# First two gate blocks on unscaled x, and a new order of events for chunks 0 and 1, in a linear attention, SwiGLU and rational kernel

## The chip, the cores and the metric

The kernel runs on one core of a Trainium2 chip. The metric is the device time of one execution in microseconds (us). Engines: PE is TensorE (matrix products), DVE is VectorE, ACT is ScalarE, POOL is GpSimd, SP is the queue of SyncE, which issues all transfers here.

## The reference

Three stages in a row, all in float32 (some inputs arrive as float64). First a linear attention over 4 batches, 8 heads, 576 positions, head size 64; then a SwiGLU block on 2304 tokens of 512 channels; then a block with a rational function.

```python
q_s = softmax(q, axis=-1); k_s = softmax(k, axis=2)
kv  = einsum('bhsd,bhse->bhde', k_s, v)
x   = einsum('bhsd,bhde->bhse', q_s, kv)      # -> [2304, 512]
rms = sqrt(mean(x * x, axis=-1) + 1e-06)
xn  = x / rms * rms_g
g   = xn @ w_gate;  val = xn @ w_val          # 512 -> 1536
y   = (g * sigmoid(g) * val) @ w_out          # 1536 -> 512
h   = y @ w_in                                # 512 -> 2048
g2  = (a0 + a1 h + a2 h^2 + a3 h^3) / (1 + |b0||h| + |b1|h^2 + 1e-06)
out = g2 @ w_out2                             # 2048 -> 512
```

## The kernel before, in words

The 2304 tokens are worked in six chunks of 384 (T). For every chunk the attention gives x, transposed, as four blocks of 128 channels; then 12 blocks f of 128 hidden channels follow, each with a gate product (g), a value product (v), Silu, the multiplication (p), and an output product (y) that adds to four PSUM banks. The results y of all chunks are parked in HBM, and after the last chunk the rational stage runs over all of them. PE does nothing but products.

Weights arrive as float64 bytes. Each weight block i (36 of them: gate, value and output of 12 blocks f) is loaded (event `l`, line 144), turned into float32 by two ACT passes (`ce`, line 181, `cl`, line 189) and a DVE join (`cj`, line 196), then split for the three-pass products into a high half (`ch`: line 219 on ACT, or line 217 on DVE for the blocks listed in HI_DVE) and a low half (`co`, line 226, on DVE, or on POOL for the blocks in LO_POOL). A product from split halves is three matmuls per 128 channels (`proj`, lines 725 to 727). In chunk 0 the gate and value products of the first NF = 4 blocks and the output products of the first NY = 8 use the joined float32 weight whole (`proj_whole`, line 738, and `y_whole`, line 754), so that they can start before the halves are made.

The events of chunks 0 and 1 stand in ORDER, a list written out by hand at the top of the file. Every name is a small function (`put`, `bank`, `reader`, from line 944 on), and each engine works its own events in the order of the list. Events of chunk 0 begin with `a`: `alk`, `alq`, `alv` load k, q, v; `akm`, `akt`, `akx`, `aks`, `akd`, `ake` are the maximum of k over the positions, its transposes and its subtraction, and the exponential; `akv` is the product of k and v (72 small matmuls) and `akn` its division; `aqm`, `aqd`, `aqe`, `aqs`, `aqn` do the softmax of q, the subtraction and the division in two halves; `axq`, `axc`, `axx` turn q and multiply it with kv for channel block p; `axo` copies x to SBUF, `axs` squares it, `arp` sums the squares over channels on PE, `arn` computes 1/rms for every token in 14 DVE instructions (`rms`, lines 574 to 593), `arb` spreads it over the partitions with a product into a PSUM bank (line 623), and `axm` (line 634) multiplies x by g and by that bank. Only then can `g0_0` begin. Events `b` and `d` are the same for the chunks 1 and 2. Events `w8`, `w9`, `w4` are groups of 8, 9 and 4 matmuls on the identity (line 936) whose result is not used.

OTHER lists events that run on the engine other than the usual one (DVE instead of POOL or ACT, or the reverse). The function `rms` and the helper lines carry the same line numbers for all chunks. PSUM has four banks (`pw`) that all `bank` events share, and four (`pa`) for y. The gate tiles `u` have two buffers, as have `uh`, `ul` and `tmp`. SP issues transfers strictly in order, so a load whose buffer is still read holds back all loads behind it: `blk1` waits for the last reader of the turned q of chunk 0, `blq` for the last `arp`, and the loads of blocks 28 to 35 for the whole weights whose buffers they take.

Of the kernel before, what the change touches and what calls it, by code (L numbers as in the profile page):

```python
# [27 lines left out]
ORDER = """
alk0 akz1 bkz1 akz0 bkz0 alq akm0 alk1 w8 akt0 alv0 akx0 aqm aks0 akd0 aqd0 alv1 ake0 aqd1 akm1 aqe w9 akv0 lg aqs l0
akt1 l1 akx1 akn0 aqn0 w4 aks1 l3 ce0 akd1 aqn1 axq1 axq0 l11 ake1 cl0 axq2 axc2 akv1 l2 cj0 axc0 axc1 ce3 ce1 l16 cl1  # L30
axx0 akn1 axx1 axs0 l4 axq3 axs1 arp0 axo0 axo1 l7 axc3 axx2 cj1 axx3 ce2 axs2 l10 arp1 axs3 ce4 arp2 axo3 blk1 axo2
arp3 cl2 arn cl4 blq ce7 ce10 ce11 ce16 cj2 w8 arb l8 cl3 axm0 axm1 axh0 l25 axm2 axh1 axm3 w4 g0_0 axh2 l19 axl1 axh3
axl0 ce8 axl2 l5 cl10 axl3 v0_0 s0_0 l9 cl7 g0_1 l15 cl16 p0_0 cj10 ce5 cj16 cl5 l21 cj4 s0_1 cj7 y0_0 ce9 l6 ce15
cl15 l13 cj3 cl9 cj5 cl11 v0_1 l12 cl8 ce6 cj11 blv0 cl6 cj15 g0_2 p0_1 ch15 ce13 co15 ce12 cj8 y0_1 s0_2 blk0 cl12
ch11 l18 cl13 cj6 ch0 co11 v0_2 ce19 l14 ch1 co0 ce21 cj9 pk0 g0_3 ch2 p0_2 ce18 cl18 lc ce14 cj12 y0_2 l20 s0_3 cj13
cl14 ch12 l17 ch13 v0_3 const co1 ch5 l23 cj14 ce20 co12 ch14 g0_4 co5 pk1 cl19 p0_3 bkm0 ce17 co14 cl17 l35 y0_3 s0_4
ce23 cj19 l24 ch10 cl21 cj18 bkt0 l26 v0_4 co13 ch18 cj17 ch4 l27 co18 ch3 g0_5 p0_4 ch17 bkm1 cl20 co4 l22 v0_5 s0_5
co10 l33 ce26 bqm ce27 co3 y0_4 l30 ce22 p0_5 cl26 co17 cl22 pk3 ce25 y0_5 ch8 bkx0 ce30 cj22 ce24 co2 bks0 ch22 bkt1
cj20 pk2 ch16 g0_6 bkx1 ch20 bqd0 bkd0 ch7 l34 bks1 s0_6 co20 v0_6 bke0 cl23 co7 g0_7 p0_6 ce34 bkd1 bqd1 ch6 y0_6
s0_7 bke1 cj23 bkv0 cj21 ch9 co6 ch23 co9 blv1 ch21 bkn0 co22 bqe co21 cl24 bqs co23 v0_7 cl27 l32 ce33 co8 cl30 g0_8  # L40
p0_7 ch19 bqn0 l31 cl25 cl33 co19 bxq0 s0_8 bkv1 cj25 bxc0 ce31 bxx0 cj27 ce32 bxq1 cj24 bxs0 y0_7 bkn1 bqn1 bxc1 ch24
bxo0 co24 ch27 v0_8 cl31 co27 ch25 cl32 bxx1 co16 ce35 p0_8 bxq2 ph0_8 bxc2 pl0_8 l29 bxs1 bxx2 cj26 bxo1 bxq3 bxa1
ch26 cj30 bxc3 co26 bxs2 bxx3 ch30 bxa2 g0_9 ce29 co25 cl29 co30 l28 s0_9 cj29 bxs3 bxo2 bxo3 v0_9 bxa3 ch29 cj32 ce28
co29 cl28 brp p0_9 g0_10 ph0_9 ch32 pl0_9 cj28 v0_10 s0_10 brn co32 ch28 co28 g0_11 p0_10 y0_8 s0_11 cj31 brb cj33
ph0_10 ch31 pl0_10 ch33 bxm0 co31 bxm1 bxh0 bxh1 bxl0 y0_9 bxm2 co33 bxm3 bxh2 bxl1 bxh3 v0_11 bxl2 bxl3 g1_0 p0_11
dlq cl34 ph0_11 pl0_11 v1_0 s1_0 cl35 cj34 g1_1 p1_0 ch34 dqm co34 v1_1 s1_1 cj35 y0_10 dqd0 ch35 p1_1 dqd1 g1_2 ph1_0
co35 dqe pl1_0 y0_11 s1_2 dqs v1_2 ph1_1 ye0_2 g1_3 ye0_1 p1_2 ye0_0 pl1_1 ye0_3 ly0 v1_3 s1_3 y1_0 p1_3 y1_1 ph1_2
dqn0 pl1_2 dxq0 ph1_3 y1_2 dxc0 pl1_3 dqn1 dxx0 dxq1 dxs0 y1_3 dxc1 dxo0 dxx1 dxq2 dxs1 g1_4 dxc2 dxa1 dxo1 dxx2 s1_4
dxq3 dxs2 v1_4 dxc3 dxa2 dxo2 g1_5 p1_4 ph1_4 pl1_4 dxx3 s1_5 y1_4 dxs3 dxo3 dxa3 drp v1_5 drn g1_6 p1_5 ph1_5 drb
s1_6 v1_6 pl1_5 dxm0 dxm1 dxh0 y1_5 dxh1 p1_6 dxl0 ph1_6 pl1_6 g1_7 dxm2 dxm3 dxh2 dxl1 dxh3 y1_6 s1_7 dxl3 dxl2 v1_7  # L50
g1_8 p1_7 ph1_7 pl1_7 v1_8 s1_8 y1_7 p1_8 ph1_8 pl1_8 g1_9 v1_9 s1_9 y1_8 p1_9 ph1_9 pl1_9 g1_10 v1_10 s1_10 y1_9
p1_10 ph1_10 pl1_10 g1_11 y1_10 s1_11 v1_11 p1_11 ph1_11 pl1_11
"""


# [1113 lines left out]
```

## Time and profile before

| | us |
|---|---|
| median of 3 runs (lowest to highest) | 950.12 (949.99 to 950.64) |
| the profiled execution, its own time | 950.66 |
| its span, first to last instruction | 948.7 |
| PE busy | 932.1 (98%) |
| DVE busy | 603.7 (64%) |
| ACT busy | 579.3 (61%) |
| POOL busy | 182.6 (19%) |
| share of PE in the chain that ended last | 95% |

Some 2 us of the execution's own time lie outside the span. Matmuls are pipelined, so a busy PE is not PE at its peak: where PE counts as busy its records can overlap, and what can be gained there shows in the start times of the products, not in the busy share. "Granted clock" (PEclk) is the share of TensorE's full 2.4 GHz that it was given; 0.50 is 1.2 GHz.

### The profile page before, as it was taken

To read this page: it belongs to the slowest core of one execution; us is meant where nothing else is said; L and a number is where in the kernel's file an instruction comes from. 1 tells how busy PE (TensorE), PEld (TensorE's weight loads), DVE (VectorE), ACT (ScalarE), POOL (GpSimd) and SP (SyncE) were. 2 spreads that over 40 slices of the span, in tenths; PEclk is the share of its full clock that TensorE was granted. 3 is DMA by queue.
4 is the path that set the end of the run, shared out by engine and by line. 5 is a ranking of instruction groups with operands and counts; after the bars stand their busy time and mean duration, and the time that the engine had idled before them with its cause. 6 is when DMAs were issued, how large, how long until landed. Compare 5 with 4: busy or idle time off the path is not lost.

```text
span 948.7 us, 13999 instructions
## 1 busy us (share of the span) xinstructions
PE 932.1 (98%) x5394; PEld 863.0 (91%) x5394; DVE 603.7 (64%) x1075; ACT 579.3 (61%) x1092; POOL 182.6 (19%) x172
## 2 busy tenths in 40 slices
PE   7999999999999999999999999999999999999998
PEld 6668899999999999999999999999999999999997
DVE  6567873415657666564623388778778778777776
ACT  3888844313653463365234578777777777777775
POOL 2014341000000000000012214224224233233221
PEclk9999999999999999999999999999999999999999
DMA  9794311013546455353398510010100100100000
GB/s 309 242 337 152 113 35 59 18 41 126 160 153 198 166 159 178 111 173 138 130 307 255 175 66 2 0 67 1 55 14 1 67 1 1 67 1 1 34 1 33
DMA packets 66705, 98.34 MB, mean 104 GB/s; under 512 B 22352, under 2 KB 48976, under 8 KB 66640
## 3 DMA queue, kind: packets, MB, share of 16 engines
q1 hardware_dynamic: 66640, 97.46, 31.6%
q8 instruction: 42, 0.69, 0.3%
q14 instruction: 23, 0.19, 0.1%
HBM read 73.33 MB, written 24.12 MB: 103 GB/s over the span
## 4 chain that ended last, share of the span: by engine, by line
PE 95%; DVE 3%; DMA 1%; ACT 1%; issue 0%; SPq 0%; POOL 0%; DVEq 0%
PE h L727 7%; PE h L725 7%; PE o L903 7%; PE o L904 7%; PE h L726 7%; PE o L902 7%; PE g L725 5%; PE g L727 5%; PE g L726 5%; PE y L727 5%; PE y L725 5%; PE y L726 5%; PE vv L725 4%; PE vv L727 4%; PE vv L726 4%; PE y L754 2%
## 5 line engine op out<-in xcount | busy, mean ns | idle before, releaser
L890 POOL TENSOR_TENSOR gl<-t,gh 128x384 fp32r<-128x384 f32 x94 | 104.7, 1114 | 252.8 <-ACT gh L888 226.9
L863 DVE SCALAR_TENSOR_TENSOR A<-S,absb,A 128x384 f32<-128x384 f32 x96 | 61.5, 641 | 93.7 <-ACT A L853 93.7
L787 ACT ACTIVATE uh<-u 128x384 fp32r<-128x384 f32 x64 | 33.6, 525 | 124.7 <-DVE u L796 89.3
L727 PE MATMUL h<-y,wf 128*128 128x384 f32 x288 | 97.2, 337 | 0.0
L725 PE MATMUL h<-y,wf 128*128 128x384 f32 x288 | 97.0, 337 | 0.0
L726 PE MATMUL h<-y,wf 128*128 128x384 f32 x288 | 96.7, 336 | 0.0
L725 PE MATMUL y<-uh,w 128*128 128x384 f32 x256 | 87.6, 342 | 0.5 <-ACT w L219 0.5
L727 PE MATMUL y<-uh,w 128*128 128x384 f32 x256 | 85.8, 335 | 0.7 <-POOL w L226 0.7
L726 PE MATMUL y<-ul,w 128*128 128x384 f32 x256 | 85.5, 334 | 0.0
L904 PE MATMUL o<-wf,gl 128*128 128x512 f32 x216 | 85.5, 396 | 0.0
L903 PE MATMUL o<-wf,gh 128*128 128x512 f32 x216 | 85.3, 395 | 0.0
L725 PE MATMUL g<-x,w 128*128 128x384 f32 x248 | 85.0, 343 | 0.0
L902 PE MATMUL o<-wf,gh 128*128 128x512 f32 x216 | 84.0, 389 | 0.0
L727 PE MATMUL g<-x,w 128*128 128x384 f32 x248 | 83.1, 335 | 0.0
L726 PE MATMUL g<-x,w 128*128 128x384 f32 x248 | 82.9, 334 | 0.0
L888 ACT ACTIVATE gh<-t 128x384 fp32r<-128x384 f32 x96 | 50.4, 525 | 46.2 <-DVE t L863 45.8
L792 POOL TENSOR_TENSOR ul<-u,uh 128x384 fp32r<-128x384 f32 x12 | 12.2, 1017 | 344.3 <-ACT uh L787 344.3
L852 ACT ACTIVATE S<-h 128x384 f32<-128x384 f32 x96 | 46.9, 488 | 30.5 <-PE h L727 28.6
L854 ACT ACTIVATE t<-h,na 128x384 f32<-128x384 f32 x96 | 64.8, 675 | 0.0
L863 DVE SCALAR_TENSOR_TENSOR t<-A,t 128x384 f32<-128x384 f32 x96 | 60.7, 633 | 0.0
L863 DVE SCALAR_TENSOR_TENSOR t<-t,na,r 128x384 f32<-128x384 f32 x96 | 59.4, 619 | 0.0
L863 DVE SCALAR_TENSOR_TENSOR t<-t,na,h 128x384 f32<-128x384 f32 x96 | 58.2, 606 | 0.0
(213 smaller groups left out, 2433.9 us busy)
## 6 DMA issues: line engine op xcount, KB each, us to landing
wf<-sd SPq DMA_DIRECT2D x36, 512.0 KB, 4.3
raw<-in_moe_w_out_dram SPq DMA_DIRECT2D x28, 511.6 KB, 4.8
sd<-ws SPq DMA_DIRECT2D x24, 512.0 KB, 2.9
raw<-in_moe_w_in_dram SPq DMA_DIRECT2D x16, 510.5 KB, 4.9
...
```

The costliest lines, as they stand in the source:

```text
L725: nc.tensor.matmul(o, lhsT=lh, rhs=rh, start=start, stop=False)
L726: nc.tensor.matmul(o, lhsT=lh, rhs=rl, start=False, stop=False)
L727: nc.tensor.matmul(o, lhsT=ll, rhs=rh, start=False, stop=stop)
L787: nc.scalar.activation(uh, u, AF.Copy)
L852: nc.scalar.activation(r["S"], h, AF.Square)
L854: nc.scalar.activation(r["t"], h, AF.Identity, scale=na[:, 3:4], bias=na[:, 2:3])
L863: nc.vector.scalar_tensor_tensor(out=out, in0=in0, scalar=scalar, in1=in1, op0=op0, op1=op1)
L888: nc.scalar.activation(r["gh"], r["t"], AF.Copy)
L890: eng.tensor_tensor(out=r["gl"], in0=r["t"], in1=r["gh"], op=ALU.subtract)
L902: nc.tensor.matmul(o, lhsT=r["gh"][:, ts], rhs=w[0], start=first, stop=False)
L903: nc.tensor.matmul(o, lhsT=r["gh"][:, ts], rhs=w[1], start=False, stop=False)
L904: nc.tensor.matmul(o, lhsT=r["gl"][:, ts], rhs=w[0], start=False, stop=last)
```

## The change

Seven parts, all in chunks 0 and 1:

- For blocks f = 0 and 1 of chunk 0 (PRE = 2) the gate and value products run on x times g without 1/rms. The spread 1/rms is copied from its bank to SBUF (`ar`, tile R); the gate is multiplied by it before Silu (`gr0_0`, `gr0_1`) and once more after it (`ur0_0`, `ur0_1`), the second time on behalf of the value.
- The products `v0_0` and `g0_0` are cut in two halves of two channel blocks (`v0_0`, `g0_0`, then `vb0_0`, `gb0_0`), and stand between the sums of squares, ahead of `arb`.
- `axo` of chunk 0 multiplies x by g on the way out of PSUM, on ACT or, for two blocks, on DVE; `axm` multiplies by 1/rms alone.
- Twelve high halves are copied by DVE (before: one), 13 low halves are made by POOL (before: 17).
- Both halves `aqd` run on POOL, `bqn0` and `bqn1` on DVE, `bxo0` to `bxo2` on DVE, `dqn1` on POOL.
- Three of the five groups of unused matmuls, and one of the two `w4`, are gone: one `w4` is left.
- ORDER is new throughout. q is loaded ahead of k; 14 weight loads (before: 9) are issued ahead of `blq`, the first load of chunk 1 that waits; `pk0` goes to the end.

```diff
-HI_DVE = (9,)
-LO_POOL = (3, 4, 5, 7, 8, 10, 14, 16, 18, 22, 23, 28, 31, 32, 33, 34, 35)
-OTHER = ('aqd1', 'axo1', 'bqn0', 'bqn1', 'dqd0', 'dqn0')
+HI_DVE = (1, 7, 9, 10, 11, 12, 15, 16, 21, 24, 25, 27)
+PRE = 2
+HALVES = (('g', 0), ('v', 0))
+LO_POOL = (1, 2, 5, 10, 14, 16, 17, 22, 23, 26, 32, 33, 34)
+OTHER = ('axo0', 'axo1', 'bxo0', 'bxo1', 'bxo2', 'dqd0', 'dqn0', 'dqn1')
 ORDER = """
-alk0 akz1 bkz1 akz0 bkz0 alq akm0 alk1 w8 akt0 alv0 akx0 aqm aks0 akd0 aqd0 alv1 ake0 aqd1 akm1 aqe w9 akv0 lg aqs l0
-akt1 l1 akx1 akn0 aqn0 w4 aks1 l3 ce0 akd1 aqn1 axq1 axq0 l11 ake1 cl0 axq2 axc2 akv1 l2 cj0 axc0 axc1 ce3 ce1 l16 cl1
-axx0 akn1 axx1 axs0 l4 axq3 axs1 arp0 axo0 axo1 l7 axc3 axx2 cj1 axx3 ce2 axs2 l10 arp1 axs3 ce4 arp2 axo3 blk1 axo2
-arp3 cl2 arn cl4 blq ce7 ce10 ce11 ce16 cj2 w8 arb l8 cl3 axm0 axm1 axh0 l25 axm2 axh1 axm3 w4 g0_0 axh2 l19 axl1 axh3
-axl0 ce8 axl2 l5 cl10 axl3 v0_0 s0_0 l9 cl7 g0_1 l15 cl16 p0_0 cj10 ce5 cj16 cl5 l21 cj4 s0_1 cj7 y0_0 ce9 l6 ce15
+akz0 alq aqm aqd0 aqd1 aqe alk0 akm0 akz1 bkz0 akt0 akx0 alk1 akm1 aks0 akd0 l10 l3 lg alv0 akt1 akx1 w4 aks1 l0 alv1
+l1 aqs akd1 ce3 ake0 akv0 ce0 cl3 akn0 aqn0 aqn1 axq1 axq0 ake1 axc1 axq2 akv1 axx1 l16 l2 axc0 cl0 axc2 ce1 cl1 cj0
+l4 l9 l7 l8 l19 l5 axx0 akn1 axx1 axs1 axs0 axq3 axc3 axx2 arp0 axx3 ce2 axo2 axs3 axo1 cj1 axo3 axo0 v0_0 arp1 arp3 ce4
+axs2 arp2 cl4 cl2 ce7 g0_0 vb0_0 gb0_0 arn arb ce5 ce10 ar cj2 g0_1 gr0_0 cj3 s0_0 ur0_0 p0_0 cj4 v0_1 gr0_1 cl5 cl10
+axm0 axm1 axm3 cj5 axm2 ce8 cl8 cj8 ce9 l6 ce6 ce16 axh1 cl16 s0_1 l11 blq blk1 l15 axh3 l13 axh0 cl7 ce15 cl6 cj10
...
@@ x_copy
+        if c == 0:
+            if f"axo{p}" not in OTHER:
+                nc.scalar.activation(
+                    st["xs", c][:, p, :], xx[:, :T], AF.Identity, scale=gk[:, p:p + 1]
+                )
+            else:
+                nc.vector.tensor_scalar(
+                    out=st["xs", c][:, p, :], in0=xx[:, :T], scalar1=gk[:, p:p + 1],
+                    scalar2=None, op0=ALU.mult,
+                )
@@ x_scaled
+        if c == 0:
+            nc.vector.tensor_tensor(out=xs, in0=xs, in1=rp[:, :T], op=ALU.mult)
+            return
@@ proj_whole, project
-    def proj_whole(o, w, x):
-        for kk in range(KD):
+    def proj_whole(o, w, x, part=range(KD)):
+        for kk in part:
...
-                proj_whole(t, W1F[which, f], st["xs", 0])
+                proj_whole(t, W1F[which, f], st["xs", 0], range(KD // 2 if (which, f) in HALVES else KD))
...
+        def project_rest(which, f, t):
+            proj_whole(t, W1F[which, f], st["xs", 0], range(KD // 2, KD))
+        def spread_copy(t):
+            st["R"] = at.tile([P, T], F32, tag="qT", name="R_0")
+            nc.scalar.activation(st["R"], t[:, :T], AF.Copy)
+        def gate_scaled(f, t):
+            nc.vector.tensor_tensor(out=gate(0, f), in0=t[:, :T], in1=st["R"], op=ALU.mult)
+        def gate_again(f):
+            u = gate(0, f)
+            nc.vector.tensor_tensor(out=u, in0=u, in1=st["R"], op=ALU.mult)
+        def silu(c, f, t):
+            u = gate(c, f)
+            nc.scalar.activation(u, u if c == 0 and f < PRE else t[:, :T], AF.Silu, scale=-1.0)
```

## Rows read from the trace of the kernel before

**Rows 1.** Busy time by stretch: us, busy of PE, PEld, DVE, ACT, POOL, PEclk, DMA share, GB/s.
```profile
0.00:37.01 37.01, 28.80 (x262) 25.16 (x263) 21.56 (x42) 17.69 (x29) 6.18 (x15) 0.91 0.83 248
37.01:90.00 52.99, 52.74 (x208) 37.09 (x207) 37.00 (x54) 44.49 (x77) 13.62 (x10) 1.00 0.88 292
90.00:134.00 44.00, 39.92 (x332) 35.30 (x331) 34.86 (x65) 33.15 (x59) 13.87 (x9) 1.00 0.20 62
134.00:943.00 809.00, 808.55 (x4591) 764.25 (x4589) 510.18 (x916) 482.20 (x926) 148.96 (x138) 1.00 0.27 87
```

**Rows 2.** PE in order of time: start us, us, instruction, count, idle before.
```profile
18.21 0.82 PE L503 MATMUL axq<-ident,qn 128*128 128x128 f32 x6
...
21.36 4.17 PE L441 MATMUL akv<-v,k 64*64 64x65 f32 x72 [1.58 <-ACT k L432]
...
30.21 2.06 PE L556 MATMUL arp<-ones,sq 128*128 128x1 f32 x18
...
35.40 0.88 PE L623 MATMUL arb<-acc,ones 128*128 128x384 f32 x2 [1.24 <-DVE acc L593]
...
37.01 2.83 PE L738 MATMUL g<-xs,whole 128*128 128x384 f32 x8
...
53.10 2.74 PE L754 MATMUL y<-u,whole 128*128 128x384 f32 x8
...
91.69 2.32 PE L441 MATMUL bkv<-v,k 64*64 64x65 f32 x72
```

**Rows 3.** DVE in order of time, the same columns.
```profile
4.61 2.09 DVE L401 TENSOR_REDUCE m<-k 128x128 f32<-128x1152 f32 x1 [3.62 <-DMA k<-in_k_dram]
...
7.74 1.75 DVE L467 TENSOR_REDUCE mq<-q 128x24 f32<-128x1536 f32 x1
9.40 1.34 DVE L427 TENSOR_TENSOR k<-k,aks 128x1152 f32<-128x1152 f32 x1
...
13.85 1.74 DVE L484 TENSOR_REDUCE sumq<-q 128x24 f32<-128x1536 f32 x1
...
16.32 1.52 DVE L417 COPY mb<-mx 128x128 f32<-128x128 f32 x1
...
32.31 0.17 DVE L574 TENSOR_REDUCE rw<-arp 128x3 f32<-128x12 f32 x1 [2.60 <-PE arp L556]
...
36.32 2.19 DVE L634 SCALAR_TENSOR_TENSOR xs<-xs,gk,arb 128x384 f32<-128x384 f32 x4 [0.47 <-PE arb L623]
```

**Rows 4.** ACT in order of time, the same columns.
```profile
11.94 1.48 ACT L480 ACTIVATE q<-q 128x1536 f32<-128x1536 f32 x1
...
20.15 1.16 ACT L432 ACTIVATE k<-k 128x1152 f32<-128x1152 f32 x1 [4.43 <-DVE k L427]
...
40.95 1.28 ACT L1083 ACT_TABLE_LOAD   x1
42.25 0.49 ACT L1083 ACTIVATE u<-g 128x384 f32<-128x384 f32 x1
```

**Rows 5.** POOL in order of time, the same columns.
```profile
9.57 1.47 POOL L475 TENSOR_TENSOR q<-q,mq 128x768 f32<-128x768 f32 x1 [7.16 <-DVE mq L467]
16.28 2.90 POOL L495 TENSOR_TENSOR qn<-q,sumq 128x768 f32<-128x768 f32 x2 [5.24 <-DVE mx L414]
```

**Rows 6.** Clock by stretch around the second product of k and v, columns as in rows 1.
```profile
20.00:21.00 1.00, 0.00 (x0) 0.00 (x0) 0.11 (x1) 0.85 (x1) 0.00 (x0) 0.68 1.01 407
...
27.00:28.00 1.00, 1.00 (x6) 0.68 (x5) 0.00 (x0) 0.60 (x2) 0.00 (x0) 0.91 0.00 0
```

**Rows 7.** The DMA queue's own waits, 0 to 130 us: total, times, longest.
```profile
SPq L362 <- PE axx L522: 13.6, 1, 13.6
```

**Rows 8.** DVE's high-half copy (line 217): ns min/median/max.
```profile
L217 DVE CAST w<-whole x1: 420/420/420, 90.1 to 90.1; 128x512 fp32r<-128x512 f32 x1
```

**Rows 9.** Groups of instructions, 40 to 130 us: busy us, mean ns of one, idle before.
```profile
L219 ACT ACTIVATE w<-tmp 128x512 fp32r<-128x512 f32 x18 | 11.0, 622 | 0.2
...
L226 DVE TENSOR_TENSOR w<-tmp,w 128x512 fp32r<-128x512 f32 x11 | 9.8, 895 | 2.0 <-ACT w L219 1.9
```

More of the change, by code (lines that the diff above doesn't have):

```diff
@@ L32 @@
-arp3 cl2 arn cl4 blq ce7 ce10 ce11 ce16 cj2 w8 arb l8 cl3 axm0 axm1 axh0 l25 axm2 axh1 axm3 w4 g0_0 axh2 l19 axl1 axh3
-axl0 ce8 axl2 l5 cl10 axl3 v0_0 s0_0 l9 cl7 g0_1 l15 cl16 p0_0 cj10 ce5 cj16 cl5 l21 cj4 s0_1 cj7 y0_0 ce9 l6 ce15
-cl15 l13 cj3 cl9 cj5 cl11 v0_1 l12 cl8 ce6 cj11 blv0 cl6 cj15 g0_2 p0_1 ch15 ce13 co15 ce12 cj8 y0_1 s0_2 blk0 cl12
-ch11 l18 cl13 cj6 ch0 co11 v0_2 ce19 l14 ch1 co0 ce21 cj9 pk0 g0_3 ch2 p0_2 ce18 cl18 lc ce14 cj12 y0_2 l20 s0_3 cj13
-cl14 ch12 l17 ch13 v0_3 const co1 ch5 l23 cj14 ce20 co12 ch14 g0_4 co5 pk1 cl19 p0_3 bkm0 ce17 co14 cl17 l35 y0_3 s0_4
@@ L37 @@
[L37 to L51, printed above, removed]
@@ L52 @@
-p1_10 ph1_10 pl1_10 g1_11 y1_10 s1_11 v1_11 p1_11 ph1_11 pl1_11
+HI_DVE = (1, 7, 9, 10, 11, 12, 15, 16, 21, 24, 25, 27)
[3 more added lines that the diff above has]
+OTHER = ('axo0', 'axo1', 'bxo0', 'bxo1', 'bxo2', 'dqd0', 'dqn0', 'dqn1')
+ORDER = """
+akz0 alq aqm aqd0 aqd1 aqe alk0 akm0 akz1 bkz0 akt0 akx0 alk1 akm1 aks0 akd0 l10 l3 lg alv0 akt1 akx1 w4 aks1 l0 alv1
+l1 aqs akd1 ce3 ake0 akv0 ce0 cl3 akn0 aqn0 aqn1 axq1 axq0 ake1 axc1 axq2 akv1 axx1 l16 l2 axc0 cl0 axc2 ce1 cl1 cj0
@@ new lines @@
+l4 l9 l7 l8 l19 l5 axx0 akn1 axs1 axs0 axq3 axc3 axx2 arp0 axx3 ce2 axo2 axs3 axo1 cj1 axo3 axo0 v0_0 arp1 arp3 ce4
+axs2 arp2 cl4 cl2 ce7 g0_0 vb0_0 gb0_0 arn arb ce5 ce10 ar cj2 g0_1 gr0_0 cj3 s0_0 ur0_0 p0_0 cj4 v0_1 gr0_1 cl5 cl10
+axm0 axm1 axm3 cj5 axm2 ce8 cl8 cj8 ce9 l6 ce6 ce16 axh1 cl16 s0_1 l11 blq blk1 l15 axh3 l13 axh0 cl7 ce15 cl6 cj10
+ur0_1 axl1 cj7 axl3 y0_0 axh2 axl2 g0_2 cj6 g0_3 cl9 ch0 cj9 v0_3 v0_2 cl15 s0_2 ce19 cj15 cj16 axl0 l21 lc ce11 ce13
+cl11 ce21 cj11 ch15 co15 ch2 l12 l25 ch11 p0_1 co11 p0_2 co0 l18 ch1 ce12 l14 l20 ch5 ch10 ce18 cl12 cl13 cj13 ce14
@@ new lines @@
+cl14 l22 l17 blk0 l23 ce20 s0_3 p0_3 const cj12 ch13 ch12 cj14 y0_1 y0_2 g0_4 co12 co1 pk1 l24 ch4 cl20 ch14 cl18 ce17
+cl19 cl17 bkm0 s0_4 cj18 co5 cj17 co13 ch17 y0_3 bkt0 v0_4 cl21 ce23 l26 l27 ch3 ce26 bkm1 p0_4 cj19 co14 g0_5 bkt1
+v0_5 ch19 s0_5 ce25 bqm ce22 cl22 ce24 co3 y0_4 p0_5 co19 co4 bkx1 y0_5 l30 l34 blv0 co17 co10 cl23 cl26 ch18 co18
+ce30 ce27 bkx0 ch7 cj22 cj20 ch8 ch22 bks0 co2 ch20 co20 bkd0 cj23 bks1 g0_6 s0_6 ch16 bqd0 co22 bqd1 v0_6 bke0 ch6
+p0_6 bkd1 g0_7 s0_7 co7 bkv0 y0_6 bke1 ch9 co6 cj21 ch21 bqe bkn0 co21 co8 co9 co16 ch23 bqs bqn0 v0_7 ce34 cl24 cl25
@@ new lines @@
+cl27 l35 pk2 l33 ce33 l32 blv1 co23 g0_8 l31 pk3 s0_8 bxq0 bxc0 ce32 bkv1 p0_7 cj25 bqn1 bkz1 bxq1 bxx0 y0_7 bxc1 bxq2
+bxx1 ce31 cj27 ch27 cj24 cl30 bxo0 co27 ch24 cj26 co24 bkn1 v0_8 ch25 cl31 ch26 bxs0 cl33 cj30 co25 p0_8 bxc2 bxq3
+bxx2 l29 ch30 ce29 ph0_8 bxc3 bxo1 co26 g0_9 bxx3 bxs1 cl29 co30 l28 s0_9 bxo2 bxa1 cj29 bxs2 ce35 cl32 bxa2 pl0_8
+v0_9 cj32 p0_9 ch29 bxs3 bxa3 co29 ch32 v0_10 brp co32 g0_11 g0_10 cl35 ph0_9 ce28 cl28 pl0_9 cj28 brn ch28 s0_11 co28
+cj31 cl34 s0_10 brb cj33 ch31 p0_10 co31 ch33 bxo3 bxm0 bxm2 y0_8 y0_9 bxm3 co33 cj35 bxm1 bxh2 bxh3 ph0_10 bxh0 bxl0
@@ new lines @@
+bxl3 bxh1 bxl1 bxl2 v0_11 dlq pl0_10 cj34 ch35 p0_11 ph0_11 pl0_11 ch34 g1_1 g1_0 v1_0 co35 co34 y0_10 y0_11 s1_0 s1_1
+dqm dqd0 p1_0 dqd1 ph1_0 pl1_0 ye0_0 dqe v1_1 p1_1 dqs v1_3 ye0_1 ye0_2 ye0_3 v1_2 g1_3 g1_2 ph1_1 y1_0 s1_3 p1_3
+pl1_1 y1_1 s1_2 dqn1 dqn0 p1_2 dxq0 ph1_2 pl1_2 ph1_3 dxc0 y1_2 dxq1 pl1_3 dxx0 y1_3 dxo0 dxc1 dxx1 dxq2 g1_4 dxc2
+dxs0 dxx2 dxq3 s1_4 dxc3 g1_7 s1_7 dxs1 v1_4 g1_6 g1_5 dxx3 dxa1 p1_4 dxo1 ph1_4 pl1_4 dxo2 dxs2 dxo3 dxa2 dxs3 s1_5
+dxa3 v1_8 drp drn v1_5 v1_6 p1_5 ph1_5 pl1_5 drb dxm3 dxm0 dxm1 dxh0 s1_6 p1_6 ph1_6 pl1_6 dxh1 dxl1 y1_4 y1_5 g1_9
@@ L53 @@
+y1_6 g1_8 g1_11 v1_7 dxm2 s1_8 p1_8 ph1_8 dxh2 dxh3 dxl0 p1_7 ph1_7 pl1_7 pl1_8 g1_10 v1_10 s1_9 s1_10 p1_10 v1_9 p1_9
+ph1_9 pl1_9 dxl2 s1_11 ph1_10 ly0 pl1_10 dxl3 y1_7 y1_8 y1_9 y1_10 v1_11 p1_11 pk0 ph1_11 pl1_11
 """
@@ L529, in x_copy @@
             st["xs", c] = big_tile(F32, st["xstag", c], f"xs_{c}").rearrange("p (c n) -> p c n", n=T)
-        if c < 3 and f"{'abd'[c]}xo{p}" not in OTHER:
+        if c == 0:
[8 more added lines that the diff above has]
+                )
+        elif c < 3 and f"{'abd'[c]}xo{p}" not in OTHER:
             nc.scalar.activation(st["xs", c][:, p, :], xx[:, :T], AF.Copy)
@@ L536, in x_square @@
         tag = "sq" if p else "acc"
-        st["sq", c] = at.tile([P, T], F32, tag=tag, name=f"sq_{c}_{p}")
+        st["sq", c, p] = at.tile([P, T], F32, tag=tag, name=f"sq_{c}_{p}")
         if p == 0:
-            st["acc", c] = st["sq", c]
-        nc.scalar.activation(st["sq", c], xx[:, :T], AF.Square)
+            st["acc", c] = st["sq", c, 0]
+        nc.scalar.activation(st["sq", c, p], xx[:, :T], AF.Square)
     def x_add(c, p, eng):
         acc = st["acc", c]
-        eng.tensor_tensor(out=acc, in0=acc, in1=st["sq", c], op=ALU.add)
+        eng.tensor_tensor(out=acc, in0=acc, in1=st["sq", c, p], op=ALU.add)
     def x_out(c, p, xx):
@@ L930, with warm @@
             nc.gpsimd.memset(t[:, :, :, D:VW], 1.0)
-        def warm(n):
-            t = pa.tile([P, 512], F32, tag="a3", name="warm")
+        def warm(n, t=None):
+            t = pa.tile([P, 512], F32, tag="a3", name="warm") if t is None else t
             for _ in range(n):
@@ L976 @@
             put(f"w{n}", warm, n)
+            put(f"x{n}", lambda n=n: warm(n, ps("warm")))
         put("lc", load_consts)
@@ L1082 @@
                     bank(f"{which}{c}_{f}", lambda t, c=c, which=which, f=f: project(c, which, f, t))
-                reader(f"s{c}_{f}", f"g{c}_{f}", lambda t, c=c, f=f: nc.scalar.activation(
-                    gate(c, f), t[:, :T], AF.Silu, scale=-1.0))
+                reader(f"s{c}_{f}", f"g{c}_{f}", lambda t, c=c, f=f: silu(c, f, t))
                 reader(f"p{c}_{f}", f"v{c}_{f}", lambda t, c=c, f=f: mult_v(c, f, t))
@@ L1088 @@
                 put(f"y{c}_{f}", project_out, c, f)
+        for which, f in HALVES:
+            reader(f"{which}b0_{f}", f"{which}0_{f}", lambda t, which=which, f=f: project_rest(which, f, t))
+        reader("ar", "arb", spread_copy)
+        for f in range(PRE):
+            reader(f"gr0_{f}", f"g0_{f}", lambda t, f=f: gate_scaled(f, t))
+            put(f"ur0_{f}", gate_again, f)
         for m in range(KD):
```

## The prediction

> **What bounds the kernel now.** I read the busy time by stretch first. From 134 us on PE is busy 808.55 of 809.00 us [rows 1]: whatever the change does in the two first chunks moves the end by as much as it moves PE there, and little behind can add or hide any of it. From 90 to 134 PE idles 44.00 - 39.92 = 4.1 us, from 37 to 90 only 0.25, and from 0 to 37.01 it idles 8.2, and some of what counts as busy there are the unused matmuls [rows 1]. So the view to read next is PE in order of time, up to the first gate product. The product of k and v for the second half of the heads ends at 21.36 + 4.17 = 25.53; the last sums of squares end at 30.21 + 2.06 = 32.27; the first gate product begins at 37.01 [rows 2]. In those last 4.7 us PE's only needed work is the spreading product of 0.88 [rows 2]: DVE computes 1/rms from 32.31 on and then scales x, whose first of four instructions begins at 36.32 [rows 3]. Ahead of 21.36 the chain is DVE's: maxima, the softmax of q, subtractions, one behind the other [rows 3].
>
> **Front, up to the second k-v product.** The order is new, so I walk it with the durations of before. k came first and had landed at 4.61 [rows 3]; q is a third larger and now first, so about 5.1 (an estimate). DVE: maximum of q 1.75, to 6.9; first maximum of k 2.09, to 8.9; its turning took from 6.70 to 7.74, here to 10.0; second maximum of k, to 12.1; subtraction 1.34, to 13.4; turning, to 13.9; sum of q with its two small followers (13.85 to the copy at 16.32, less 0.3 for another step) 2.2, to 16.1; second subtraction, to 17.5 [rows 3]. One half of q's subtraction has left DVE; POOL does both, 2 x 1.47 from 6.9 to 9.8 [rows 5], ACT's exponential of q follows, 1.48, to 11.3 [rows 4], well ahead of the sum. ACT's exponential of k, 1.16, ends at 18.7 [rows 4]. POOL's divisions of q, 2.90 [rows 5], run from 16.1 to 19.0. PE's first k-v product can begin at about 15.0, behind the one `w4` that is left and a transpose.
>
> What the k-v products cost hangs on the clock. At half clock the 72 matmuls took 4.17, at full clock 2.32 [rows 2]. The clock fell in 20 to 21 us, after PE had paused, and was back in 27 to 28, about 6 us after the products that began at 21.36, with no unused matmul among them [rows 6, 2]. In the new order PE works without pause from about 12.6, so I take the rise at 18.6: the first k-v product then does 3.6/4.17 of itself at half clock and the rest in 0.3, to 18.9; three turnings at 0.41 (0.82 for two [rows 2]), to 20.1; the second k-v product, 2.32, to 22.5. That is 3.0 earlier than 25.53.
>
> **From there to the sums.** The same copies, squares, products and sums follow, paced by ACT with two conversions of weights among them. I keep their length, 32.27 - 25.53 = 6.7, which puts the last sum at 29.2; the multiplication by g rides on the copies. The new half of `v0_0` stands inside that stretch, where PE waits for ACT.
>
> **The RMS root.** Six products, from 37.01 to 53.10, took 16.09, or 2.68 each, 1.34 a half [rows 2]; this holds the small wait ahead of the first y. After the sums PE now has three halves, 4.0, to 33.2. 1/rms needs 32.31 to 35.40 = 3.1 [rows 3, 2], to 32.3, so it is covered with 0.9 to spare, and the spreading product ends at 34.1. `g0_1`, `v0_1`, `y0_0` and `g0_2` follow, 10.7, to 44.8. Before, the same six products were done at 53.10: **a lead of 8.3**.
>
> The waits that this adds: `s0_0`, and behind it on ACT the conversions of weights 5, 10 and 8, waits for the copy of R (0.49, sized by the Silu) and `gr0_0` (0.55, a quarter of 2.19) after the spreading product; then a table load of 1.28, Silu 0.49, `ur0_0` and `p0_0`, 0.55 each [rows 3, 4]: 34.1 + 3.9 = 38.0, and DVE's join of weight 3 and 4 beside it, 38.7. `y0_0` is due at 34.1 + 5.4 = 39.5, so 0.8 is left; without the cover of `g0_1` and `v0_1` it would cost 4.6. `axm` now waits until `v0_1` has read the unscaled x; behind it on DVE stand the joins of weights 5 and 8, and `g0_2` waits for it. y0_0's 2.7 cover the first scaling. Both edits I put at nothing.
>
> **SP and the loads.** Before, SP stood 13.6 us at the first load of chunk 1, until the turned q was read [rows 7], with nine weights issued. Now 14 are ahead of that stop, so the transfers that run dry there do not; `pk0`, moved to the end past every load, is not needed before chunk 2. The weights that a lead of 8.3 asks for earlier are thus there earlier. The loads of v now come behind two weights: at the stretch's mean of 248 GB/s [rows 1] the 3.6 MB up to the first v take 14.5 us and the 4.7 MB up to the second 19.0, ahead of the products at 15.0 and 20.1 by 0.5 and 1.1. This is the thinnest cover here; if it is gone, a us late costs a us. I put both at nothing.
>
> **37 to 134.** PE waits 4.3 here [rows 1]. ACT is the busier neighbour: 44.49 of 52.99 in the first part [rows 1]. Eleven more high halves leave it, 11 x 0.622 = 6.8 [rows 9]. DVE takes them at 0.420 [rows 8], 4.6; four more low halves at 0.895 [rows 9], 3.6; four multiplications by R at 0.55, 2.2; the two divisions of q of chunk 1, 0.9 each from the subtraction of 1152 elements in 1.34, 1.8; three copies of x at 0.55, 1.7: 13.9 in all [rows 3]. DVE goes from 71.9 to 85.8 in a stretch that PE needs 97.0 - 4.3 = 92.7 for. The waits are bounded by 0, both engines ahead at every product, and by 4.3 + 13.9 - 6.8 = 11.4, all that DVE gains and ACT doesn't lose. I take 4.3 again, the row itself: relief and load stand against each other. The other moves between POOL and DVE (`bxo`, `dqn1`, chunk 1's order) lie beside PE's full stretch.
>
> One row speaks against the copies on DVE: a copy of 128 elements took 1.52 while POOL multiplied from 16.28 on [rows 3, 5]. The Trainium skill, "GPSIMD Engine Reference", section "Specifications", says that POOL shares its SBUF interface with VectorE and contends with VectorE's two-port instructions and those with two SBUF inputs; the trace agrees. If each of the eleven copies met a POOL instruction so, 11 x 1.3 = 14 more would stand on DVE; POOL loses six instructions, so I count none.
>
> **Sum.** The profiled execution took 950.66, 2.0 around its span included, 0.54 over the median of 950.12. 950.66 - 8.3 + 0 = 942.4; against the median, **941.8**. A measurement of this kernel tells 0.2%, 1.9 us, from no change.
>
> **Rivals.**
> *No waits left* (0.12). ACT's relief ends the 4.3: 937.5. For it: the waits of rows 1 stand where ACT is late. Against: DVE.
> *DVE becomes the bound* (0.20). DVE idled 25 of 97 us, in order, for others. If two thirds of that, 16.7, remain beside 85.8, it needs 102.5, PE waits 9.8, 5.5 more than before: 947.3. At 20 us of remaining idle the lead is used up. For it: the load; against: much of that idling is for PE's own products, and ends when DVE is late.
> *The lead is given back* (0.06): converted weights come no earlier than before, PE runs into them by 90 us, and the end stays, 950.1. For it: ACT was 84% busy; against: five loads more ahead of SP's stop.
> *The clock stays low* (0.10), the rival on the slower side. Four of five unused groups are gone; if PE's short products with pauses don't bring the clock back until the three halves are done, the first k-v product costs 0.3 more, the turnings 1.2, the second 1.85, the x products (one channel block each, so a quarter of 2.68) and the sums 2.7 + 2.06, four halves 5.4: 13.5 more, 955.3. It decides from 8.3 us of full-clock work done at half clock, that is, if the clock is still low when the half of `v0_0` begins. For it: the fall at 20 to 21 after pauses. Against: the return by 28 on the same products alone [rows 6]. The Trainium skill, "TensorE: Matmul & The Clock Gate", section "What's actually happening", states that throttled is the default and activity releases it; by that rule taking filler work away is a loss, and the trace agrees that the clock falls after pauses.
>
> **Chances.** Forecast 0.52, and the rivals as given. Faster: 0.52 + 0.12 + 0.20 = 0.84; same 0.06; slower 0.10. The range reaches from no waits, 937.5, to just beyond the DVE case, 948.5; it leaves out the two last.
>
> **What would show it.** Second k-v product done near 22.5; sums near 29; no pause of PE over 0.5 between the sums and `g0_2`; `y0_1` or its neighbours beginning near 45; PE idle from there to the first product of chunk 1 about 4; PE full behind. Wrong if the granted clock is 0.50 beyond 20 us, if `y0_0` waits for `p0_0`, or if PE's waits from 45 to 125 exceed 8.

## The result, and the profile after

The changed kernel took **936.18 us** (median of 4 runs, 935.64 to 936.32) against 950.38 for the kernel before in the same job (949.99 to 950.99): a ratio of 0.9849, 95% interval 0.9832 to 0.9866. It is faster by 14.2 us, where 8.3 were forecast, and lies 1.3 below the lower end of the range. The profiled span is 934.5 (948.7 before).

The busy times on the page of the changed kernel: engine, us, share of the span, instructions.

```profile
PE 918.8 (98%) x5336; PEld 852.8 (91%) x5336; DVE 608.0 (65%) x1098; ACT 571.7 (61%) x1078; POOL 177.4 (19%) x168
```

The busy time by stretch of the changed kernel, columns as in [rows 1]. Ahead of the clock's first recorded change, here at 18.50 us, the PEclk column shows 1.00; the start times tell more, 108 ns for each pair of small matmuls of the first k-v product up to 18.50 and 58 ns from there on, so PE had half its clock until then.

```profile
0.00:26.00 26.00, 14.42 (x184) 12.17 (x185) 15.81 (x25) 12.25 (x18) 7.35 (x15) 1.00 0.98 303
...
37.01:80.00 42.99, 42.99 (x176) 31.14 (x175) 40.68 (x64) 37.74 (x68) 14.67 (x10) 1.00 0.87 282
80.00:121.00 41.00, 41.00 (x346) 37.94 (x345) 38.27 (x79) 31.11 (x55) 6.02 (x6) 1.00 0.30 84
121.00:930.00 809.00, 808.60 (x4588) 763.89 (x4587) 508.62 (x914) 481.79 (x925) 149.40 (x138) 1.00 0.27 87
```

From 37.01 to 121 PE is busy in every moment, where it idled 4.3 us from 37 to 134 before [rows 1]. DVE is busy 40.68 + 38.27 = 78.95 of 84, or 94%, and PE doesn't wait for it once. The last row is the full stretch behind, the same as before.

PE in order of time in the changed kernel, columns as in [rows 2]:

```profile
15.35 3.75 PE L443 MATMUL akv<-v,k 64*64 64x65 f32 x72
...
20.35 2.32 PE L443 MATMUL akv<-v,k 64*64 64x65 f32 x72
...
26.28 1.45 PE L753 MATMUL v<-xs,whole 128*128 128x384 f32 x4
27.57 2.06 PE L568 MATMUL arp<-ones,sq 128*128 128x1 f32 x18
29.50 1.54 PE L753 MATMUL g<-xs,whole 128*128 128x384 f32 x4
30.87 1.45 PE L753 MATMUL v<-xs,whole 128*128 128x384 f32 x4
32.16 1.45 PE L753 MATMUL g<-xs,whole 128*128 128x384 f32 x4
33.45 0.81 PE L635 MATMUL arb<-acc,ones 128*128 128x384 f32 x2
34.10 2.74 PE L753 MATMUL g<-xs,whole 128*128 128x384 f32 x8
...
39.26 2.74 PE L769 MATMUL y<-u,whole 128*128 128x384 f32 x8
41.84 5.32 PE L753 MATMUL g<-xs,whole 128*128 128x384 f32 x16
...
118.71 0.33 PE L740 MATMUL g<-x,w 128*128 128x384 f32 x1
```

The last row is the first product of chunk 1. In the kernel before it is this one:

```profile
133.01 0.33 PE L725 MATMUL g<-x,w 128*128 128x384 f32 x1
```

The x8 of such a product on whole weights is four matmuls, one for each channel block, with two records each.

The three half products stand between the sums (from 27.57) and the spreading product (33.45), where PE waited (1.24 ahead of the spreading product) or did unused matmuls before [rows 2]. No row has an idle time. (In ORDER of the changed kernel `axx1` stands once, behind `akv1`.) `g0_2`, the first eight of the sixteen records from 41.84, is done at 41.84 + 2.58 = 44.42; the same six products were done at 53.10 before, so the lead there is **8.68**. The first product of chunk 1 begins at 118.71, at 133.01 before. From `g0_2` to it PE took 74.29 instead of 53.10 to 133.01 = 79.91: another **5.62**. Behind it both kernels take the same, 934.5 - 118.71 = 815.79 and 948.7 - 133.01 = 815.69. The two gains, 14.3, are the difference of the spans, 14.2.

The 5.62 are the pauses of PE from 53.10 to 133.01 in the kernel before, all of which are gone. Their records sum to 4.1. That kernel's waits of PE from 37 to 134: who waited for what, us in total, times, longest (the last of them, ahead of the first y, lies before 53.10 and so in the lead):

```profile
PE bxx L522 <- ACT qT L512: 1.3, 2, 0.6
PE v L725 <- ACT w L219: 0.8, 1, 0.8
PE v L727 <- DVE w L226: 0.8, 1, 0.8
PE y L727 <- POOL w L226: 0.7, 1, 0.7
PE y L725 <- ACT w L219: 0.5, 1, 0.5
PE y L754 <- DVE whole L196: 0.3, 1, 0.3
```

A pause costs more than its record says. PE of the kernel before at the second of the two ahead of `bxx`, in order of time, then of the changed kernel at a place with the same three steps and no pause:

```profile
111.18 0.49 PE L503 MATMUL bxq<-ident,qn 128*128 128x128 f32 x3
112.31 0.92 PE L522 MATMUL bxx<-qT,kv 128*128 128x192 f32 x4 [0.64 <-ACT qT L512]
112.93 0.47 PE L725 MATMUL g<-x,w 128*128 128x384 f32 x1
```

```profile
99.07 0.49 PE L505 MATMUL bxq<-ident,qn 128*128 128x128 f32 x3
99.40 0.82 PE L524 MATMUL bxx<-qT,kv 128*128 128x192 f32 x4
99.92 0.47 PE L740 MATMUL g<-x,w 128*128 128x384 f32 x1
```

From the start of the turnings to the start of what follows `bxx` it is 112.93 - 111.18 = 1.75 before and 99.92 - 99.07 = 0.85 after: 0.90 for a pause with a record of 0.64, or 0.26 more. Six pauses at 0.26 more are 1.5, which is what lies between 4.1 and 5.62.

### The profile page after: what moved, and what is told of

It is laid out like the page before. It is cut to its first block, busy times and chain, and to the rows that moved or that the text cites. A ratio compares the mean times of both kernels' runs of the same rounds, so it can differ in the third digit from the quotient of the medians.

```text
span 934.5 us, 13877 instructions
## 1 busy us (share of the span) xinstructions
PE 918.8 (98%) x5336; PEld 852.8 (91%) x5336; DVE 608.0 (65%) x1098; ACT 571.7 (61%) x1078; POOL 177.4 (19%) x168
## 4 chain that ended last, share of the span: by engine, by line
PE 98%; DVE 1%; DMA 1%; ACT 0%; issue 0%
PE h L742 7%; PE h L740 7%; PE o L918 7%; PE o L919 7%; PE h L741 7%; PE o L917 7%; PE g L740 5%; PE g L742 5%; PE g L741 5%; PE y L742 5%; PE y L740 5%; PE y L741 5%; PE vv L742 4%; PE vv L740 4%; PE vv L741 4%; PE y L769 2%
```

## Experiments

All variants are of the changed kernel unless "before" is said. Its 936.18 is the mark; the kernel before took 949.75 to 950.62 in the jobs of these runs, so differences under a us between jobs carry no weight.

**1. The old high halves.** `HI_DVE = (9,)`: eleven copies go back to ACT.

> The changed kernel with one thing undone: eleven of the twelve high halves go back from VectorE to ScalarE, in the same places of the order. Theory 'balance' (PE's 4.3 us of waits between 37 and 134 us went because ScalarE was relieved of 6.8 us): ScalarE is late again at the products of blocks 7 to 9, PE waits 2 to 5 us between 75 and 120 us, time 938.5 to 941. Theory 'order' (they went because the new list puts products between the short turns and x products and draws conversions forward): PE waits under 1 us, time 936 to 937. Theory 'supply' (five more loads are issued ahead of SP's stop): as 'order', 936 to 937.

939.41, ratio 0.9868 to 0.9898: 3.2 worse. PE's longest new wait is for ACT (columns as in the waits above):

```profile
PE v L740 <- ACT sq L552: 1.3, 1, 1.3
```

'Balance' gave this size. The longest wait is for a square of chunk 1 on ACT, not for a weight. From the end of `g0_2` to the first product of chunk 1 PE takes 77.77 (74.29 in the changed kernel): all of the loss lies there.

**2. The old lists in the new order** (of `OTHER` the entries for chunk 0 stay as changed).

```diff
-HI_DVE = (1, 7, 9, 10, 11, 12, 15, 16, 21, 24, 25, 27)
+HI_DVE = (9,)
-LO_POOL = (1, 2, 5, 10, 14, 16, 17, 22, 23, 26, 32, 33, 34)
+LO_POOL = (3, 4, 5, 7, 8, 10, 14, 16, 18, 22, 23, 28, 31, 32, 33, 34, 35)
-OTHER = ('axo0', 'axo1', 'bxo0', 'bxo1', 'bxo2', 'dqd0', 'dqn0', 'dqn1')
+OTHER = ('axo0', 'axo1', 'bqn0', 'bqn1', 'dqd0', 'dqn0')
```

> The changed kernel with all engine lists of chunks 0 and 1 as before (one high half on VectorE, 17 low halves on GpSimd, divisions of q of chunk 1 on GpSimd, copies of x of chunk 1 on ScalarE), only the two scaled copies of chunk 0 stay on VectorE; the order is the new one. 'Balance': more than in the kernel with the old highs alone, PE waits 3 to 7 us between 70 and 125 us, time 939 to 943. 'Order' and 'supply': waits under 1.5 us, time 936 to 938.

946.90, ratio 0.9951 to 0.9976: 10.7 worse, more than expected. PE's largest waits, and the stretch behind the first:

```profile
PE g L742 <- POOL w L228: 3.9, 1, 3.9
PE v L740 <- DVE kv L463: 1.4, 1, 1.4
```

```profile
93.40:96.80 3.40, 3.06 (x10) 3.07 (x11) 2.71 (x2) 0.00 (x0) 2.41 (x3) 0.50 0.76 281
```

PE pauses for a low half on POOL, and for the 3.4 us behind the pause it is granted 0.50 of its clock (1.2 GHz), so the products behind the wait are slow too. But the waits for `bxx` of the kernel before don't appear: the order alone has ended those.

**3. The new lists in the old order** (the kernel before with `HI_DVE` and `LO_POOL` of the change, and `OTHER` with its entries for chunks 1 and 2).

> The kernel before, in its old order and with the RMS root first, with the engine lists of chunks 0 and 1 of the changed one (twelve high halves on VectorE, 13 low halves on GpSimd, and so on). 'Balance': PE's waits of 1.6 us at 94 to 97 us and 1.2 at 126 to 129 go, those of 1.3 at 110 to 113 may stay: 947 to 948.5. 'Order': the waits stay within 1 us of 4.3, 949.5 to 951, or grow, since the old order puts the copies where VectorE is busy. 'Supply': 949.5 to 951.

951.22 against 950.62, ratio 1.0000 to 1.0017: no gain. PE's waits behind the front:

```profile
PE v L727 <- DVE w L226: 1.6, 1, 1.6
...
PE bxx L522 <- ACT qT L512: 1.3, 2, 0.6
PE y L727 <- DVE w L226: 1.0, 2, 0.6
```

The waits for ACT's copies have shrunk to one, and waits for DVE's low halves stand in their place. 'Order' is nearest. The 3.7 by which run 2 still beats the kernel before (950.62 - 946.90) are not the order's worth behind the front, for run 2 also has the half products and the whole new front. What bears on that is PE's time from the end of `g0_2` to the first product of chunk 1, the same products in all four profiled runs:

| us | old order | new order |
|---|---|---|
| old lists | 79.91 | 84.86 (run 2) |
| new lists | 82.23 (run 3) | 74.29 |

Either part alone makes this stretch longer, by 2.3 and by 5.0; both together make it 5.6 shorter. Run 3's time hides its 2.3, since in its profiled run the clock was back at 24.6 us instead of 27.2 and `y0_0` began 1.1 earlier. Its pause of 1.6 was also followed by 3.4 us at 0.50.

**4. The root first.** `PRE = 0`, `HALVES = ()`: x is scaled by 1/rms before `g0_0`, as before the change: in ORDER `axm` stands ahead of `g0_0`, `v0_0` behind it, and the copy of R with its multiplications is gone; the rest is the changed kernel's.

> The changed kernel with the RMS root applied first again: no half products among the sums, gate and value of blocks 0 and 1 read scaled x, the copy of R and the four multiplications by it are gone; all else in the new order, as near as the dependences allow. Theory 'cover' (the root's 3.1 us on VectorE and the scaling stood on PE's path and the half products cover them): PE does nothing needed but the spreading product for 3.9 us longer between the sums and the first gate product, and the half product among the sums comes behind: 4.5 to 5.5 us more, 940.7 to 941.7. Rival 'slack' (the new order's later stretch would take up the delay, since converted weights are then further ahead): under 2 us more, 936.5 to 938.

944.08, ratio 0.9918 to 0.9943: 7.9 worse, more than the 4.5 to 5.5 expected. The waits, and the stretch in which they fall:

```profile
PE arb L635 <- DVE acc L605: 3.0, 1, 3.0
PE g L753 <- DVE xs L647: 0.6, 1, 0.6
```

```profile
26.00:37.00 11.00, 6.73 (x25) 4.42 (x24) 6.16 (x21) 6.02 (x10) 0.00 (x0) 0.61 1.09 326
...
28.00:29.00 1.00, 0.86 (x6) 0.86 (x6) 0.00 (x0) 1.00 (x3) 0.00 (x0) 0.74 1.06 384
29.00:30.00 1.00, 0.29 (x2) 0.20 (x1) 0.61 (x5) 0.72 (x2) 0.00 (x0) 0.50 1.09 384
```

The wait is the one the prediction named. The clock is the rest: its mean is 0.61 in this stretch, and it stood at 0.50 from 28.5 to 38.7. It fell while PE still did the sums of squares, ahead of the wait of 3.0, which begins at 29.3.

**5. The root first, with its pauses filled** (run 4 with 13 unused matmuls ahead of the spreading product, 3 behind it and 3 ahead of `g0_0`).

> The kernel with the RMS root first in the new order, now with 19 unused matmuls again while PE waits for the root and for the scaling (13, 3 and 3). Without them the clock fell to 0.50 from 28.5 to 38.7 us and the time was 944.1, 7.9 more than the changed kernel. Theory 'root and clock' (5.2 us of it are PE's waiting for the root, the rest is the clock): the clock stays at 1.00, first y product about 5.2 later than in the changed kernel, 941 to 942. Rival 'root alone' (the clock costs nothing because PE would wait for conversions anyway): 943.5 to 944.5 at full clock.

941.77, ratio 0.9898 to 0.9925: 5.6 worse than the changed kernel, and the clock, which fell in run 4, stays at 1.00 there; `y0_0` begins at 44.77, 5.5 later than its 39.26. So of run 4's 7.9 the root itself is 5.6 and the clock 2.3. 'Root and clock' holds. In the changed kernel the half products stand where run 5 has unused matmuls, and the clock stays up as well, so the change could leave those out. The Trainium skill, "TensorE: Matmul & The Clock Gate", section "What's actually happening", says that throttled is the default and activity releases it; these two runs agree.

**6. The old low halves.** `LO_POOL` alone as in run 2.

> The changed kernel with one list undone: GpSimd makes the 17 low halves of before instead of 13, in the new order; high halves and all else as changed. With all lists undone the time was 946.9, with the high halves alone undone 939.4, so 7.5 us lie with the low halves, the divisions of q of chunk 1 and the copies of x. Theory 'low halves' (GpSimd, at 1.3 us or more each, is late with blocks whose due place in the new order was set for VectorE): most of it is here, PE waits 3 us or more on a low half made by GpSimd, 940 to 944. Rival 'divisions' (the two divisions of q on GpSimd hold up the low halves behind them): under 2 us here, 936 to 938.

938.96, ratio 0.9865 to 0.9892: 2.8 worse, between the theories. No product waits for a low half of POOL; the largest wait is for a load of v, 1.0 by its record at `bkv`. The stretch behind `g0_2` takes 77.83 for 74.29.

**7. The old divisions.** `bqn0` and `bqn1`, the divisions of q of chunk 1, back on POOL.

> The changed kernel with one thing undone: the two divisions of q of chunk 1 go back to GpSimd (3.4 us there, about 2 on VectorE). 'Divisions': the turns of q and the low halves behind them on GpSimd are late, PE waits 2 to 5 us between 80 and 105 us, 938 to 942. 'Low halves': under 1.5 us more, 936 to 937.5.

941.22, ratio 0.9889 to 0.9916: 5.0 worse; 'divisions' had the size. The wait, and POOL in order of time just before it:

```profile
PE g L742 <- POOL w L228: 3.5, 1, 3.5
```

```profile
88.06 1.47 POOL L497 TENSOR_TENSOR qn<-q,sumq 128x768 f32<-128x768 f32 x1 [8.14 <-ACT raw L191]
89.49 1.71 POOL L228 TENSOR_TENSOR w<-tmp,w 128x512 fp32r<-128x512 f32 x1
```

The same low half in the changed kernel, where nothing stands ahead of it:

```profile
86.28 1.31 POOL L228 TENSOR_TENSOR w<-tmp,w 128x512 fp32r<-128x512 f32 x1 [6.00 <-ACT w L221]
```

One division of 1.47 stands in the queue ahead of the low half that `g0_8` needs, and it can't begin at 86 itself: the sum of q that it divides by is ready on DVE only at 87.88 (its last step, `L488`, runs from 87.58 for 0.30). So the low half begins 3.2 later, and PE pauses 3.5; then the clock is at 0.50 for 3.4 us. POOL was idle for 8.14 before the division: it isn't the work of the engine that matters but what stands ahead of the late instruction, and what that waits for. Runs 1, 6 and 7 add up to 3.2 + 2.8 + 5.0 = 11.0, run 2's 10.7; run 2 also moves the copies of x.

**8. Six more high halves on DVE** (weights 4, 13, 17, 18, 20 and 22 added to `HI_DVE`).

> The changed kernel with six more high halves copied by VectorE instead of ScalarE (weights 4, 13, 17, 18, 20, 22), the order as it is. VectorE was busy 78.95 of the 84 us from 37 to 121 without one wait of PE; six copies of 0.42 add 2.5 and make it 81.5, 97%; ScalarE loses six of 0.62, 3.7 us. Theory 'fit' (the waits of PE are set by where each instruction stands in its engine's queue, and the lists fit this order): most of these weights are then late or in the way of others, PE waits 1 to 5 us in all, 937.5 to 942. Rival 'load' (what counts is how much work each engine has): VectorE still has 2.5 us to spare, so no wait of PE over 0.3 us comes between 37 and 121, 935.5 to 937. Rival 'bound' (VectorE at 97% is the limit): waits of several single products spread over the whole stretch, above 942.

937.06, ratio 0.9845 to 0.9878: 0.9 over the mark. The stretch from 37 to 121, in which the changed kernel has 78.95 for DVE and 68.85 for ACT:

```profile
37.01:121.00 83.99, 83.71 (x514) 67.82 (x513) 80.13 (x146) 64.99 (x114) 20.67 (x15) 1.00 0.56 178
```

At 95% DVE still nearly keeps up: PE idles 0.28 there by its records, and from the end of `g0_2` to chunk 1 it takes 75.47 for 74.29. 'Bound' falls, and 'fit' overrates how exactly the lists must match; 'load' is nearest (its upper end was 937). Moving copies to ACT hurts by 3.2, moving six more to DVE hardly does.

**9. Fewer early loads.** The loads of weights 8, 19, 5, 6 and 11 go behind the stop of SP at `blq blk1`.

> The changed kernel with only nine weight loads ahead of SP's first waiting load, as before: five (blocks 8, 19, 5, 6, 11) go behind the loads of k and q of chunk 1. Theory 'supply' (the earlier loads are part of why PE does not wait): the transfers run dry for some microseconds near 25 to 30 us, conversions are late, PE waits 2 us or more between 37 and 60 us, 938 to 942. Theory 'engines' (conversions are paced by ScalarE and VectorE, not by transfers): within 1 us of the changed kernel, 935.5 to 937.2.

947.46, ratio 0.9951 to 0.9978: 11.3 worse, more than both theories had. ACT in order of time around its largest wait, then the wait of PE that comes of it:

```profile
43.01 1.19 ACT L183 ACTIVATE raw<-raw 128x512 f32<-128x512 uint8 x2 [13.10 <-DMA raw<-in_moe_w_gate_dram]
44.10 0.47 ACT L1079 ACTIVATE R<-arb 128x384 f32<-128x384 f32 x1
```

```profile
45.81 5.34 PE L753 MATMUL v<-xs,whole 128*128 128x384 f32 x8 [9.09 <-DVE whole L198]
```

The conversion of weight 5 (`ce5`) stands in ACT's queue ahead of the copy of R, so a late load of one weight holds up the scaling of the first gate. On DVE the join of weight 3, which `v0_1` needs, stands behind that scaling, and there PE stands for 9.1. The clock falls in this wait, to 0.50 from 40.6 to 50.9 us, and `v0_1` takes 5.34 instead of 2.74: of the 11.7 by which `y0_0` comes later (50.99 for 39.26), 9.1 are the wait and 2.6 the clock. In the changed kernel this wait is there too, but short:

```profile
32.42 1.26 ACT L183 ACTIVATE raw<-raw 128x512 f32<-128x512 uint8 x2 [2.40 <-DMA raw<-in_moe_w_gate_dram]
34.30 0.49 ACT L1079 ACTIVATE R<-arb 128x384 f32<-128x384 f32 x1 [0.62 <-PE arb L635]
```

The load is there 0.6 us before it would delay R (R waits 0.62 more for the spreading product).

**10. Four fewer early loads** (run 9, but weight 5 stays early).

> The changed kernel with four weight loads (blocks 8, 19, 6, 11) behind the loads of k and q of chunk 1, block 5 left ahead. With five behind, ScalarE stood 13 us at the conversion of block 5 with the copy of R queued behind it, and the time was 947.5. Theory 'queue position' (only a load whose conversion stands ahead of R on ScalarE costs that much): the first y product begins within 0.5 of 39.3 us, and the time is 936 to 938. Rival 'supply' (the dry stretch of the transfers itself makes all later conversions late): PE waits 4 us or more between 40 and 60 us, 940 to 945.

938.61 (937.56 to 940.52), ratio 0.9870 to 0.9900: 2.4 worse, with a wide spread. In the profiled run of 937.56, `y0_0` begins at 39.14 and one new wait of PE is left:

```profile
PE v L753 <- DVE whole L198: 1.2, 1, 1.2
```

So 8.9 of run 9's 11.3 hung on the load of weight 5 alone, by its conversion's place in a queue and the clock that fell in the wait; four weights that come later cost the rest. 'Queue position' is nearest; 'supply' is not reached.

**11. More early loads in the kernel before** (weights 8, 25, 19, 5 and 9 ahead of `blk1`).

> The kernel before with five more weight loads (blocks 8, 25, 19, 5, 9) ahead of SP's first waiting load, nothing else changed. 'Supply alone': the transfers no longer run dry at 26 to 31 us, PE's waits of 4.3 us shrink by 1 to 4, 946 to 949. Rival 'no use without the lead' (with the first gate product at 37 the weights are in time anyway, and the waits behind are ScalarE's and VectorE's): 949.5 to 951.

949.29 against 950.33, ratio 0.9982 to 1.0000: at the edge of what can be told. In the profiled run the stretch from `g0_2` to chunk 1 is 79.93, as before (79.91); what it gains lies ahead of `y0_0`, where in this run the clock was back at 24.9 us instead of 27.2. Early loads are a condition of the lead, not a gain.

**12. A busier front** (`w20`, `w4`, `w4` and `w7` around the first steps, and the second k-v product ahead of `axq2`).

> The changed kernel with 31 more unused matmuls while PE waits for the first maxima (20 ahead of the first transpose, then 4, 4 and 7 in place of 4), and the second product of k and v one place ahead of the last turn of q. The clock rose only at 18.5 us in the changed kernel; here it should be up before the first k-v product at 15.3. Theory 'clock in front' : first k-v product 2.3 instead of 3.7, the second begins when the exponential of k is done, about 19.1 instead of 20.4, all behind 0.8 to 1.2 earlier, 935.0 to 935.6. Rival 'paced by the others' (PE is not what the next step waits for; GpSimd's divisions and ScalarE are): under 0.4, 935.8 to 936.6.

935.94 (935.81 to 936.01), ratio 0.9836 to 0.9863: not to be told from the changed kernel. PE in order of time:

```profile
15.15 2.32 PE L443 MATMUL akv<-v,k 64*64 64x65 f32 x72 [0.29 <-issue]
...
19.00 2.32 PE L443 MATMUL akv<-v,k 64*64 64x65 f32 x72
...
24.76 0.80 PE L568 MATMUL arp<-ones,sq 128*128 128x1 f32 x6 [0.69 <-ACT qT L514]
...
27.44 2.06 PE L568 MATMUL arp<-ones,sq 128*128 128x1 f32 x18
```

Both k-v products run at the full clock, the second ends 1.35 earlier (21.32 for 22.67), and the last sums begin only 0.13 earlier (27.44 for 27.57): PE now waits for ACT's copies of the turned q. 'Paced by the others' holds.

## Why the prediction was right and wrong

**What bounds the kernel: right.** From chunk 1's first products on both kernels take the same within 0.1, and so do all twelve variants (815.7 to 815.8).

**The front: right in its numbers, half right in its reason, and lucky in one.** The second k-v product was to end at 22.5 and did at 22.67; the clock was to rise at 18.6 and did at 18.50; the sums were to end at 29.2 and did at 29.63. That the rise came within 0.1 is luck: in the nine runs below that have the same matmuls up to there (1, 2 and 4 to 10) it came at 16.35 to 18.27. It mattered little: in the runs among these that keep the front as it is (1, 2, 6, 7, 8 and 10) `y0_0` began at 38.82 to 39.14, for 39.26 here. And run 12 shows that the k-v product was not what set the sums: 1.35 gained there is worth 0.13 behind it. Keeping the 6.7 from it to the sums was right for this version only, in which ACT and PE come out nearly together.

**The root: right.** The spreading product was to end at 34.1 and did at about that; `y0_0` 39.5 and 39.26, `g0_2` 44.8 and 44.42. The two edits "at nothing" cost nothing: `y0_0` had 1.5 us to spare. Run 5 prices the root alone at 5.6; the prediction's lead of 8.3, less the 32.27 - 29.2 = 3.1 that it gave the front, is 5.2. Runs 4, 5 and 9 lose all that they lose ahead of the end of `g0_2`: from there to chunk 1 they take 74.15 to 74.20, as the changed kernel does (74.29), so nothing behind takes up a delay of the front.

**SP and the loads at nothing: the price right, the cover misjudged.** The two loads of v landed at 13.96 and 18.68, 1.4 and 1.7 us ahead of the products that read them (0.5 and 1.1 had been forecast). The thinnest cover was not v but weight 5, ahead of R in ACT's queue, with 0.6 to spare (run 9: 11.3 if it is late). The text named what stands behind the first Silu on ACT, but not `ce5`, which stands ahead of the copy of R.

**37 to 134: the step that failed.** "I take 4.3 again, the row itself: relief and load stand against each other". It was 0, and by the lengths of the stretch 5.62 were gained. Two errors lie in it:
- It set busy times against each other, ACT's 6.8 less against DVE's 13.9 more, where the waits stood at single steps. Of the recorded 4.1, 1.3 were `bxx2` and `bxx3` waiting for the turned q just behind its turning. The new order puts other work between: `bxx1`, `v0_8` and `bxq3` ahead of `bxx2`, and `bxx2` and `g0_9` ahead of `bxx3`, so PE has work while ACT copies. This wait is gone with the old lists too (run 2) and there with the new lists in the old order (run 3). The prediction put chunk 1's order "beside PE's full stretch" and didn't walk it. The rest, waits for halves of weights, ends only with lists and order together: either alone lengthens the stretch (runs 2 and 3); which moved event ended which of these waits wasn't taken apart further.
- It took the idle record for the cost. Six pauses with 4.1 of records were worth 5.62, and the one shown above 0.90 for 0.64. So even the 'no waits' rival, 937.5, was 1.3 high; that, not another gain, put the result outside the range.

**The rivals.** *No waits left* was what happened, at a chance of 0.12. *DVE becomes the bound* fell: DVE was busy 94% of the stretch with no wait, and run 8 added copies with hardly any cost. Of DVE's 25 us of idling two thirds were to remain; 5 of 84 did. *The lead is given back* fell, but run 9 gives back 11.3 of the 14.2 by a load alone. *The clock stays low* fell: it rose ahead of the half of `v0_0`. The price of copies was right, 0.42 in eleven of twelve and 0.77 in the other in the changed kernel; DVE's low halves took 0.685 at the median, not 0.895, so its added load was also overrated (78.95 in the stretch, where 85.8 had been summed). The contention beside POOL that the Trainium skill, "GPSIMD Engine Reference", section "Specifications", names did occur, but rarely: one copy of twelve, and three low halves of 23 (1.35 to 1.78), each beside an instruction of POOL.
